# A ConvNeXt V2 block: one ring of four PSUM banks for the expansions, a new order inside the slot, and another pace of the recompute

## The chip, the cores and the metric

The kernel runs on one core of a Trainium2 chip. The core has five engines, each with its own instruction stream: TensorE (PE; its weight loads are a row of their own, PEld), VectorE (DVE), ScalarE (ACT), GpSimd (POOL) and SyncE (SP), which only issues transfers here. Matmuls write PSUM[...]; ACT and DVE read it. The engines wait for each other through semaphores. The metric is the time of one execution on the device in microseconds.

## The reference

The input is an image of 512 x 512 pixels with 96 channels in bf16.

```python
out = sum(xp[:, i:i+H, j:j+W, :] * dw[i, j] for i in range(3) for j in range(3))  # depthwise 3x3
h = layernorm(out)                          # over the 96 channels of each pixel
h = gelu(einsum('bhwc,ce->bhwe', h, w1))    # expansion to 384 channels
gx = sqrt((h * h).sum(axis=(1, 2)) + 1e-6)  # over ALL pixels, per channel
nx = gx / (gx.mean(axis=-1) + 1e-6)
h = grn_gamma * (h * nx) + grn_beta + h
return x + einsum('bhwe,ec->bhwc', h, w2)
```

The sum over all pixels in `gx` divides the work in two: no output can be made before every pixel has been expanded.

## The kernel before, in words

The image is cut into 128 blocks (`NBLK`) of four rows, 2048 pixels each. A block's pixels form four quarters of 512.

**Phase 1** walks through the blocks in slots (`for s in range(last_slot + 1)`, line 721). The convolution of block s runs in slot s; its normalisation follows some slots later, by way of statistics on PE, a Newton iteration on POOL and a trip through DRAM; and in most slots an earlier block is expanded (the "mlp" of that slot). There are 128 such expansions. The first few stand among slots that only convolve, then 114 in all have a convolution beside them, and the last 14 have none, because the convolutions have run out. Within a slot the order on each engine is the order in which the code calls the stages, since `InOrder` (line 22) keeps each engine's instructions in program order.

- The convolution of a block (`conv_taps`, line 408) is three bursts of 24 small matmuls into a tile Y of three banks. The first two bursts end in a `drain` of PE (line 441). `evac` copies Y to `y_bf` on ACT. In some early slots without expansion (`spare`) the result goes to two U tiles instead of Y.
- The expansion (`mlp_units`, line 611) makes twelve banks of 512 columns: `pair(j)` two quarters of 128 channels each, kept as `gsh`, for three groups of channels; `rest(n)` the remaining 3072 columns, kept as `gm`. A unit is some matmuls into a U tile followed by one GELU on ACT that empties it. `psU` has two buffers of two banks, so a unit's first matmul waits for the GELU of the unit before the last.
- Of the channel-major part (`gsh`, and the first 1536 columns of `gm` in two blocks of three), DVE takes the squares' sums with `bn_stats` (`squares`, `squares_rest`). The rest is pixel-major, and PE takes its squares as a Gram matrix (`gram_mms`, line 664): 12 matmuls in two blocks of three, 24 in the third, mostly one slot after the expansion.
- `stage_stats` makes the sums for the normalisation on PE; `stage_moments`, `stage_rstd`, `stage_newton` follow in later slots. Squares `ysq` and normalised `yn` are made on POOL.

Only the first quarter of `gsh` of a block is stored to DRAM (`g_dram`). The last two blocks stay resident.

**Phase 2** (from line 847) starts when the sums are complete and walks over the blocks again. Per block it adds the bias to x on POOL (`stage_xb`), recomputes the three quarters that weren't stored in three units (`recompute_units`: three matmuls into a tile U2, one GELU of 1536 columns), multiplies with the scaled w2 (`stage_mm2`, four sub-blocks of 12 matmuls each into O), adds on DVE and stores. The recompute of later blocks is mixed in between the sub-blocks by `pace` (line 330): it may run ahead by an allowance that starts at `LEAD` = 8 units and grows evenly, and at the end of each block it must at least have finished the next one. The six recompute units of the two resident blocks are made at the end of Phase 1, in `psU` (lines 843 to 845).

## Time and profile before

| | us |
|---|---|
| median of 11 runs | 1565.86 (one run of 7031.4, the others 1563.43 to 1570.16) |
| the profiled execution | 1567.04 |
| its span in the profile | 1565.3 |
| Phase 1 with convolution beside the expansion | about 114 to 945 |
| Phase 1 without convolution | about 945 to 1023 |
| Phase 2 | about 1032 to 1563 |

| engine | busy us | share of the span |
|---|---|---|
| PE | 1453.5 | 93% |
| ACT | 1446.9 | 92% |
| POOL | 1313.9 | 84% |
| DVE | 1129.8 | 72% |

The profile is of one execution. A busy PE is not PE at its peak, since matmuls overlap and their ends are modelled; the start of one to the start of the next says more. A group's row gives the busy time, the mean length of one instruction in nanoseconds, the idle time of its engine before it, and whose end finished most of that idle time. "PEclk" is the share of its full clock that TensorE was granted.

### The profile page before, as it was taken

What the parts mean: (1) busy time and instruction counts of PE and PEld (TensorE: products, weight loads), DVE (VectorE), ACT (ScalarE), POOL (GpSimd) and SP (SyncE); (2) the same over time, 40 slices, a digit from 0 to 9 for tenths busy, and PEclk for the clock granted to TensorE, in tenths of its full rate; (3) what the DMA queues carried; (4) which work ended last, traced back from release to release, by engine and by line L of the source; (5) the groups of instructions that cost most, each with busy time, mean ns of one, the idle gap of its engine ahead of it and who ended that gap; (6) DMA issues with size and microseconds to landing.
All of it is one profiled execution on the core that took longest, in us unless ns stands there. A gap on an engine that the chain in (4) does not pass through costs nothing. (4 is left out here: it accounts for less than half of the span.)

```text
span 1565.3 us, 55720 instructions
## 1 busy us (share of the span) xinstructions
PE 1453.5 (93%) x23749; PEld 844.7 (54%) x23749; DVE 1129.8 (72%) x2027; ACT 1446.9 (92%) x1306; POOL 1313.9 (84%) x933
## 2 busy tenths in 40 slices
PE   7889999999999999999999997789999999999997
PEld 3434444444444444444444444367777777777765
DVE  6738978889888888889888888855555555555544
ACT  3879999999999999999999999999999999999996
POOL 3558898988989898898889887559999999999994
PEclk8989999999999999999999999999999999999999
DMA  5668687787778778777778767779999999999993
GB/s 146 183 180 257 206 262 236 226 252 222 231 237 250 230 240 250 221 234 236 249 214 248 223 188 226 258 252 388 392 386 391 392 391 388 380 386 387 381 368 149
DMA packets 235470, 427.94 MB, mean 273 GB/s; under 512 B 34102, under 2 KB 148374, under 8 KB 235222
## 3 DMA queue, kind: packets, MB, share of 16 engines
q1 hardware_dynamic: 219972, 356.59, 70.2%
q0 software_dynamic: 13888, 67.64, 11.4%
q8 instruction: 186, 3.05, 0.8%
q14 instruction: 62, 0.51, 0.1%
q10 hardware_dynamic: 1362, 0.15, 0.1%
HBM read 272.78 MB, written 150.72 MB: 271 GB/s over the span
## 5 line engine op out<-in xcount | busy, mean ns | idle before, releaser
L32 PE MATMUL U<-ynT,w1p 128*128 128x512 bf16 x2166 | 602.1, 380 | 43.5 <-ACT gm L32 8.1
L32 DVE BATCH_NORM_STATS2 bst<-gsh 128x6 f32<-128x512 bf16 x756 | 468.8, 673 | 129.4 <-ACT gsh L32 128.8
L32 ACT ACTIVATE gr<-U 128x1536 bf16<-128x1536 f32 (+1 forms) x384 | 521.0, 1450 | 15.9 <-PE U L32 13.9
L32 POOL TENSOR_TENSOR yn<-y_bf,rbc 128x1536 bf16<-128x1536 bf16 x128 | 397.0, 3104 | 89.2 <-ACT rbc L32 30.4
L32 DVE TENSOR_TENSOR o_sb<-O,xb 128x384 bf16<-128x384 f32 x512 | 277.7, 557 | 252.0 <-PE O L32 180.1
L278 POOL TENSOR_TENSOR xb<-xr,B2c 128x1536 f32<-128x1536 bf16 x126 | 394.9, 3135 | 42.2 <-DVE B2c L32 34.0
L32 ACT ACTIVATE gsh<-U 128x1024 bf16<-128x1024 f32 x378 | 369.4, 1024 | 55.5 <-ACT gm L32 29.9
L32 ACT ACTIVATE gm<-U 128x1024 bf16<-128x1024 f32 x384 | 367.9, 1036 | 0.1
L32 PE MATMUL Y<-xT,Wq 64*32 64x511 bf16 (+1 forms) x8694 | 323.1, 391 | 9.3 <-DVE B2bc_f L32 3.7
L32 POOL TENSOR_TENSOR ysq<-y_bf 128x1536 bf16<-128x1536 bf16 x114 | 313.3, 2749 | 12.6 <-ACT y_bf L32 12.2
L32 PEld LDWEIGHTS <-w1p 128*128 128x128 bf16 x2166 | 169.1, 97 | 277.2 <-issue 173.1
L32 PEld LDWEIGHTS <-gr 128*128 128x128 bf16 x4584 | 228.6, 98 | 84.5 <-ACT gr L32 12.1
L32 PE MATMUL O<-W2s,gr 128*128 128x96 bf16 x4584 | 251.4, 206 | 12.1 <-ACT gr L32 9.4
L32 PEld LDWEIGHTS <-Wq 64*32 64x32 bf16 x9216 | 102.6, 91 | 189.6 <-issue 149.8
L32 PE MATMUL U<-w1p,ynT 128*128 128x384 bf16 (+2 forms) x1032 | 161.4, 272 | 34.1 <-ACT gm L32 31.0
L32 ACT ACTIVATE y_bf<-Y 128x1536 bf16<-128x1536 f32 x121 | 175.1, 1447 | 19.1 <-PE Y L32 18.9
L32 DVE STREAM_TRANSPOSE xT<-xin 128x576 f32<-128x576 f32 (+1 forms) x256 | 181.4, 748 | 5.9 <-PE Y L32 2.9
L32 DVE BATCH_NORM_STATS2 bst<-gm 128x6 f32<-128x512 bf16 x252 | 156.5, 677 | 0.9 <-ACT gm L32 0.9
L32 PEld LDWEIGHTS <-ynT 128*128 128x128 bf16 x1032 | 88.6, 96 | 91.4 <-issue 69.9
L32 PE MATMUL SG<-gm 128*128 128x128 bf16 x2064 | 136.3, 219 | 0.5 <-ACT gm L32 0.3
L32 PEld LDWEIGHTS <-gm 128*128 128x128 bf16 x2064 | 120.9, 98 | 11.5 <-issue 0.5
L250 POOL DMA_DIRECT2D xr<-in_x_dram x123 | 67.6, 549 | 27.6 <-POOL xb L278 27.6
(103 smaller groups left out, 702.7 us busy)
## 6 DMA issues: line engine op xcount, KB each, us to landing
ynT<-yn_dram SPq DMA_DIRECT2D x254, 384.0 KB
xin<-in_x_dram SPq DMA_DIRECT2D x126, 432.0 KB
yn_dram<-yn SPq DMA_DIRECT2D x512, 96.0 KB
xr<-in_x_dram POOLq DMA_DIRECT2D x128, 384.0 KB, 6.6
out_dram<-o_sb SPq DMA_DIRECT2D x127, 384.0 KB
g_dram<-gsh SPq DMA_DIRECT2D x126, 384.0 KB
gl<-g_dram SPq DMA_DIRECT2D x84, 384.0 KB
gl<-g_dram POOLq DMA_DIRECT2D x42, 384.0 KB, 6.6
```

The costliest lines, as they stand in the source:

```text
L32: r = f(*a, **k)
L250: pq.dma_start(out=xr[:], in_=x[0, r0:r0 + GR].rearrange("r w c -> (r w) c").rearrange("(p g) c -> p g c", g=PXP))
L278: pq.tensor_tensor(out=xb[:], in0=grp[q]["xr"][:], in1=bias[:, None, :].to_broadcast([128, PXP, C]), op=ALU.add)
```

## The change

There are four edits.

1. The two U buffers of two banks become one tile `ring` of four banks, allocated once. `banks(n)` returns the next n neighbouring banks of it, from the start again where they wouldn't fit. All users of `psU` take their banks from there: the expansions, the spare convolutions, `stage_spread`, the six resident recompute units.
2. `pair` and `rest` become `unit(bank, n)`, an expansion of one or two banks. The second pair and the last one are split into two single banks, so a slot with convolution has four units of two banks and four of one, with one GELU each.
3. The order inside a slot is another. With convolution: the Gram matmuls of the block before come in two halves between expansions; the evacuation of the convolution stands behind the fourth two-bank step, `unit(6, 2)`, where it stood behind `pair(2)`; the statistics come at the end; the drain after the second burst is gone. Without convolution: the Gram matmuls come after the second pair.
4. `pace` lets the allowance grow by `total` over the whole of Phase 2, not by `total + 2 - LEAD`.

```diff
-        psU = p1.enter_context(tc.tile_pool(name="psU", bufs=2, space=bass.MemoryType.PSUM))
+        psU = p1.enter_context(tc.tile_pool(name="psU", bufs=1, space=bass.MemoryType.PSUM))
+        NB = 4
+        ring = psU.tile([128, NB, W], f32, name="U")
+        next_bank = [0]
+
+        def banks(n):
+            k = next_bank[0] % NB
+            if k + n > NB:
+                k = 0
+            next_bank[0] = k + n
+            return ring[:, k:k + n, :]
...
-                    U = psU.tile([128, 2, QW], f32, name="U")
+                    U = banks(2)
...
-            even = LEAD + (n * NSUB + sub + 1) * (total + 2 - LEAD) / (NSUB * NBLK)
+            even = LEAD + (n * NSUB + sub + 1) * total / (NSUB * NBLK)
...
-                Ua = psU.tile([128, 2, W], f32, name="U")
-                Ub = psU.tile([128, 2, W], f32, name="U")
+                Ua, Ub = banks(2), banks(2)
...
-                if n < 2:
+                if n < 2 and fence:
                     pe.drain()
...
-            def pair(j):
-                U = psU.tile([128, 2, QW], f32, name="U")
-                for t in range(2):
-                    cm_mm(U[:, t, :], j, t)
-                act.activation(out=gsh[:, :, j, :], in_=U[:], func=ACTF.Gelu_apprx_tanh)
-
-            def rest(n):
-                U = psU.tile([128, 2, QW], f32, name="U")
...
+            def unit(bank, n):
+                U = banks(n)
+                if bank < 2 * NCH:
+                    j, t0 = divmod(bank, 2)
+                    for t in range(t0, t0 + n):
+                        cm_mm(U[:, t - t0, :], j, t)
+                    act.activation(out=gsh[:, t0:t0 + n, j, :], in_=U, func=ACTF.Gelu_apprx_tanh)
+                    return
...
-        def gram_mms(b):
-            for k in range((TAIL - px0(b)) // E):
+        def gram_mms(b, part=None):
+            n = (TAIL - px0(b)) // E
+            for k in range(n) if part is None else range(n // 2) if part == 0 else range(n // 2, n):
...
-                conv(0)
-                pair(0)
-                pair(1)
...
-                squares(0)
-                conv(1)
-                spread_out()
...
-                pair(2)
-                squares(1)
...
-                conv(2)
-                if evac:
+                if taps:
+                    conv(0)
+                    unit(0, 2)
+                    unit(2, 1)
+                    squares(0)
+                    conv(1, False)
+                    spread_out()
+                    if s + 2 < NBLK:
+                        turn_x(s + 2)
+                    unit(3, 1)
+                    unit(4, 2)
+                    squares(1)
+                    gram_of_last(0)
+                    unit(6, 2)
+                    squares(2)
+                    for k in get("turn"):
+                        stage_turn(k)
+                    conv(2)
                     evac()
-                rest(0)
-                squares(2)
...
-                rest(1)
...
-                rest(2)
-                squares_rest()
+                    gram_of_last(1)
+                    unit(8, 2)
+                    unit(10, 1)
+                    unit(11, 1)
+                    squares_rest()
+                    for b2 in get("stats"):
+                        stage_stats(b2)
+                else:
+                    unit(0, 2)
+                    unit(2, 2)
+                    spread_out()
+                    gram_of_last(0)
+                    gram_of_last(1)
+                    squares(0)
+                    unit(4, 2)
...
+                    unit(10, 2)
+                    squares_rest()
```

## The prediction

> **What bounds the kernel now.** I read the page's slices first: from about 110 us to 1023 us TensorE (PE) and ScalarE (ACT) are both nearly full, and after 1032 us too. A table of stretches then separates four stages (busy us of PE, PEld, DVE, ACT, POOL, each with its count; then clock, DMA share, GB/s):

> ```profile
> 114.00:945.00 831.00, 777.73 (x14078) 390.51 (x14075) 713.38 (x1210) 777.27 (x774) 736.74 (x558) 1.00 0.77 234
> 945.00:1023.00 78.00, 57.73 (x472) 33.26 (x470) 67.52 (x114) 74.52 (x81) 44.00 (x33) 1.00 0.80 259
> 1032.00:1466.00 434.00, 430.93 (x6094) 315.03 (x6094) 232.37 (x434) 430.25 (x318) 406.19 (x246) 1.00 1.02 381
> 1466.00:1563.00 97.00, 86.35 (x1183) 61.27 (x1179) 46.28 (x85) 84.12 (x61) 75.07 (x42) 1.00 0.79 289
> ```

> The first is Phase 1 with a convolution in every slot (PE 94%, ACT 94%); the second has no convolution left and is ACT's (96%); the third is Phase 2, PE and ACT at 99%; in the fourth ACT falls to 87%. The starts of the first GELU of each slot give the period: 7.45, 7.45, 7.64 us and again, mean 7.52, in Phase 1; 5.78 us on average in the 14 slots without convolution. The timeline of PE in one slot (start, duration, count; the bracket is idle time before it):

> ```profile
> 601.80 0.87 PE L32 MATMUL Y<-xT,Wq 64*32 64x512 bf16 x24
> 602.79 1.03 PE L32 MATMUL U<-ynT,w1p 128*128 128x512 bf16 x4
> 603.75 0.87 PE L32 MATMUL Y<-xT,Wq 64*32 64x512 bf16 x24
> 604.74 0.60 PE L32 MATMUL U<-ynT,w1p 128*128 128x512 bf16 x2
> 605.27 0.90 PE L32 MATMUL Y<-xT,Wq 64*32 64x512 bf16 x24
> 606.10 0.61 PE L32 MATMUL U<-w1p,ynT 128*128 128x384 bf16 x4
> ...
> 607.59 0.83 PE L32 MATMUL SG<-gm 128*128 128x128 bf16 x12
> 608.73 0.60 PE L32 MATMUL U<-w1p,ynT 128*128 128x256 bf16 x4 [0.31 <-ACT gm L32]
> ```

> PE stands back to back and waits for ACT once, 0.3 us. It can, because the two U buffers let it fill one while ACT empties the other.

> For the change the hand-over between them matters. It shows bare where ACT has nothing else, after the last slot: PE writes a pair, ACT empties it.

> ```profile
> 1018.86 0.59 PE L32 MATMUL U<-ynT,w1p 128*128 128x512 bf16 x2
> 1019.49 1.02 ACT L32 ACTIVATE resg<-U 128x1024 bf16<-128x1024 f32 x1 [0.62 <-PE U L32]
> 1020.57 0.60 PE L32 MATMUL U<-w1p,ynT 128*128 128x128 bf16 x4 [0.68 <-ACT resg L32]
> ```

> Start of a pair to start of its GELU: 0.63 us here, 0.69 at 602.79 with 603.48 on ACT; I take 0.66. The GELU takes 1.02, and PE starts 0.05 us after its end (1019.49+1.02=1020.51, 1020.57). So a pair handed over **in series** costs 0.66+1.02+0.05 = 1.73 us; a single bank, with one matmul of 0.215 us less and 512 columns of ACT, 0.45+0.59+0.05 = 1.09. The 0.59 is from:

> ```profile
> L32 ACT ACTIVATE y_bf<-Y 128x1536 bf16<-128x1536 f32 x121 | 175.1, 1447 | 19.1 <-PE Y L32 18.9 <-issue 0.2
> L32 ACT ACTIVATE y_bf<-U 128x512 bf16<-128x512 f32 x7 | 4.1, 591 | 0.0
> ```

> [...] its halved stretches are 6.83, 3.41 and 10.24 us long, whole windows. I measured each window's share of streaming from the matmul starts (512 columns each 0.215 us, eight convolution matmuls at once counted as one). All three windows that lost the clock streamed 0.30 or less; none at 0.38 or more did before the end. At half clock 0.69, 0.81 and 0.85 restored it, 0.65 and 0.68 did not. Two of these windows (clock is the third number from the end):

> ```profile
> 85.70:89.10 3.40, 1.77 (x48) 0.63 (x48) 0.00 (x0) 1.48 (x1) 2.78 (x1) 1.00 0.40 147
> 89.10:92.50 3.40, 3.28 (x79) 1.19 (x64) 1.75 (x5) 2.47 (x2) 1.54 (x5) 0.51 0.30 71
> ```

> **The change part by part.** (1) *The ring.* One tile U of four banks replaces two tiles of two banks. In the built program the first matmul of every unit waits for the ACTIVATE directly before it: u2 (bank 2) for u0's (banks 0 and 1), u3 (bank 3) for u2's, u4 for u3's, and so on; before, each waited for the last but one. Dependencies are kept for the tile, not for its banks. So PE and ACT take turns, and each slot becomes one chain. With t=0 at u0's first matmul:

> - u0 0, evacuated by 1.68, u2 1.73; evacuated 2.77.
> - The second burst runs 0.31 after u2's start (as 604.96 to 605.27) for 0.83: u3 at 2.87, evacuated 3.91; u4 3.96, evacuated 5.64; u6 5.69, evacuated 7.37.
> - The third burst fits behind u6; y_bf starts on ACT at 7.3 and holds it 1.35 (next start at 606.32 to 607.66): ACT is free at 8.65. Second Gram half and u8's matmuls are done by then, so u8's GELU runs 8.65 to 9.67.
> - u10 9.72, evacuated 10.76; u11 10.81.
> - Behind u11's matmuls stand the statistics (0.60, from 606.55 to 607.15) and the first burst of the next slot with its drain (0.99): 10.81+0.22+0.60+0.99 = 12.6.

> **12.6 us against 7.52, at full clock.** The slots without convolution are six pairs in series, 6 x 1.73 = 10.4 plus 0.1 for long Gram blocks, against 5.78.

> (2) *Clock.* In this chain PE streams little. From u8 to the end of u11's matmuls (7.5 to 11.1) it streams 0.43+0.21+0.21 us, 0.13 to 0.28 of any window lying there: below every window that lost the clock before. At half clock I work the chain out again with a pair's second matmul at 0.43 and a matmul's length of 0.61 (pair 1.13 to ACT, single 0.70), bursts of 1.39 and 1.54 (90.54 to 95.15 is three): 17.3 us. There the stretch from u4 to u8 streams over 0.69 of a window, so the clock comes back once a slot, to be lost again near u11 or, where a block has 24 Gram matmuls, later. Following the window's edges through a few slots gives 15 to 16.7; I take **15.4** as mean. Without convolution no cold window reaches 0.69: six pairs at 2.20 and Gram of double length make 13.7.

> (3) *Splits of two pairs into singles*: two more ACTIVATEs a slot, price inside the chain. (4) *Evacuation behind the fourth expansion*: y_bf comes one unit later; it hides u8's matmuls. POOL's square of it and the norm come slots later, DVE and POOL have over 5 us more per slot, so nothing waits there. (5) *Gram halves*: 0.35 or 0.70 us each, nothing, because ACT's 1.02 us on u4 and the burst behind u6 cover them; without that cover 0.7 or 1.4. (6) *Statistics at the end*: on the chain, 0.60, counted; the moments on DVE come after them in the next slot as before. (7) *Second drain gone*: bursts with it take 0.98, without 0.83 (605.27 to 606.10): saves 0.15, of which the chain feels at most 0.1. DMA queues are not reordered within a slot.

> (8) *Pace of Phase 2.* The allowance grows by 384/512 instead of 378/512 a sub-block, so the lead no longer runs out. Before, lead minus need is 4.95 - 0.047n units and is gone at block 105. The last output addition of each block shows that: mostly 4.0 to 4.2 us apart until 1470 us, then 4.46, 4.64 and 5.53. PE there waits for a GELU inside the block. Twenty blocks from 1469.9 to 1562.1 took 92.2; at 4.10 they take 82, and I count **11 us** gained with the tail, between 5 and 18: POOL needs 3.13 (xb) + 0.55 (xr's issue) + gaps, 4.0 a block, and sets the floor.

> Sum on the profiled execution (span 1565.3, 1567.0 around it; the median of runs, 1565.86, is a microsecond less):

> - 114 slots with convolution x (15.4-7.52) = +898
> - 14 slots without x (13.7-5.78) = +111
> - six resident recompute pairs in series +8, first stages (spare convolutions, spreads through one ring) +5
> - Phase 2 -11

> 1567+1011 = 2578; I say **2580**.

> **The rivals.** *B: serial at full clock.* If ping-pong at this rate counts as busy, 114 x 5.08 = 579, 14 x 4.7 = 66, +6 +5 -11: **2212**. For it: pairs every 0.92 us at 1024 us kept the clock at 0.44 to 0.47 streaming. Against: the new chain has windows at half of that. *C: cold almost throughout*: 114 x 9.8 + 111 + 2: **2795**; against it the dense stretch u4 to u8. *D, the other side: PE is let in as soon as its own banks are free.* Then the ring works as a finer double buffer. Place: the first matmul of each unit; price: a slot is PE's own work, 7.45-0.44-0.15 = 6.86, or 7.49 with 24 Gram matmuls, mean 7.07, so 114 x -0.45 - 11 gives **1505**. It decides from the point where a unit waits for the ACTIVATE before last; the built program waits for the last, which is why I give it little.

> **How the numbers follow.** A 0.65, B 0.22, C 0.10, D 0.03. A spreads from 14 to 16.7 us a slot, 2400 to 2740. The range takes in B's lower side and A's upper: 2205 to 2760. Differences within 0.2% (3 us) can't be told from none by these runs: faster 0.03 from D, same 0.01, slower 0.96.

> **What would show it.** U matmuls waiting for ACT and ACT for U about seven times a slot, over 3 us a slot each; slots of 12.6 (B) or 15 to 16.7 (A); a mean clock near 0.7 from 100 us on (A), 0.99 (B); DVE and POOL near half busy; Phase 2 of about 519 us with no block above 4.7. Slots near 7 us, or U's matmuls starting while the previous unit's ACTIVATE runs, would make all of it wrong; a clock that follows another measure than streaming moves me between B and C.

## The result and the profile after

The changed kernel takes **2500.87 us** (median of 8 runs, 2494.42 to 2502.09) against 1566.0: 1.596 times as long, interval 1.594 to 1.598. The forecast was 2580, range 2205 to 2760. The profiled execution has a span of 2499.1 us and a mean granted clock of 0.779.

The table of stretches of the changed kernel (busy us of PE, PEld, DVE, ACT, POOL, each with its count; then clock, DMA share, GB/s) has Phase 1 with convolution, Phase 1 without, and Phase 2:

```profile
150.00:1765.00 1615.00, 1125.08 (x13996) 481.11 (x13993) 741.52 (x1195) 847.97 (x981) 732.00 (x544) 0.73 0.38 119
1765.00:1950.00 185.00, 105.48 (x553) 56.59 (x551) 76.76 (x120) 89.67 (x89) 44.89 (x33) 0.57 0.36 115
1967.00:2496.00 529.00, 514.79 (x7272) 374.38 (x7271) 278.09 (x516) 511.78 (x377) 482.94 (x287) 1.00 1.00 365
```

ACT was at 94% in the first stretch and is at 53% now, PE fell from 94% to 70%, and the clock is at 0.73. Phase 2 is as long as before. The table of waits says what stands in between (total us, times, longest):

```profile
ACT gsh L32 <- PE U L32: 589.1, 490, 3.3
PE U L32 <- ACT gm L32: 291.2, 271, 1.7
PE U L32 <- ACT gsh L32: 285.1, 330, 1.4
ACT gm L32 <- PE U L32: 270.7, 384, 1.4
```

In the kernel before the same waits were these; the fourth, of `gm` for PE, is not in the list, and all idle time in front of these GELUs was 0.1 us:

```profile
PE U L32 <- ACT gm L32: 39.7, 112, 1.3
ACT gsh L32 <- PE U L32: 23.8, 46, 0.6
PE U L32 <- ACT gsh L32: 5.2, 11, 0.7
```

Now PE waits for ACT 576 us and ACT for PE 860 us: they take turns. The starts of the matmuls say the same without a wait being put down to anyone. In the 110 slots with convolution that the table below counts, the changed kernel's trace has 1832 matmuls into U, and not one starts while ACT reads U. Before, 1153 of 1829 do.

The timeline of PE in a slot that ran at full clock up to its last unit:

```profile
1624.71 0.60 PE L32 MATMUL U<-ynT,w1p 128*128 128x512 bf16 x2
1626.48 0.38 PE L32 MATMUL U<-ynT,w1p 128*128 128x512 bf16 x1 [1.16 <-ACT gsh L32]
1626.79 0.88 PE L32 MATMUL Y<-xT,Wq 64*32 64x512 bf16 x24
1627.60 0.39 PE L32 MATMUL U<-ynT,w1p 128*128 128x512 bf16 x1
1628.67 0.59 PE L32 MATMUL U<-ynT,w1p 128*128 128x512 bf16 x2 [0.69 <-ACT gsh L32]
...
1630.38 0.59 PE L32 MATMUL U<-ynT,w1p 128*128 128x512 bf16 x2 [0.78 <-ACT gsh L32]
...
1634.39 0.38 PE L32 MATMUL U<-w1p,ynT 128*128 128x256 bf16 x2 [1.66 <-ACT gm L32]
1635.45 0.58 PE L32 MATMUL U<-w1p,ynT 128*128 128x128 bf16 x2 [0.69 <-ACT gm L32]
...
1636.59 1.48 PE L32 MATMUL Y<-xT,Wq 64*32 64x512 bf16 x24
```

From the first line on, the units start at 1.77, 2.89, 3.96, 5.67, 9.68 and 10.74 us; the forecast's chain had 1.73, 2.87, 3.96, 5.69, 9.72 and 10.81. The last line is the first burst of the next slot at half clock: 1.48 us where it took 0.87.

```profile
1604.40:1607.80 3.40, 1.38 (x19) 1.00 0.84 262
1607.80:1611.20 3.40, 3.01 (x48) 0.51 0.03 10
...
1614.60:1618.00 3.40, 2.71 (x17) 0.50 0.00 0
1618.00:1621.50 3.50, 2.35 (x41) 0.99 0.93 294
```

PE's busy time is more than what it streams, which is counted here as in the prediction. The first holds units 10 and 11 with their waits and streams less than 0.3 of the window; the third holds units 4 and 6 and half of a long Gram block at half clock, and streams 0.82.

| stage | before, us | after, us | change | forecast |
|---|---|---|---|---|
| start to the first steady slot (first GELU of `gm`) | 114.4 | 143.8 | +29 | +36 |
| 110 slots with convolution | 829.9 | 1633.2 | +803 | +867 |
| 14 slots without, resident recompute, sums | 89.4 | 191.2 | +102 | +119 |
| Phase 2, first to last addition | 528.5 | 526.8 | -2 | -11 |

(Starts in the trace; of the forecast, four of the 114 slots and the 5 us of the first stages are put to the first row.) The mean slot with convolution is 14.85 us where 15.4 was forecast, the one without 12.9 where it was 13.7.

### The profile page after: what moved, and what is told of

Its sections match the earlier page's. It is cut to its first block, busy times and chain, and to the rows that moved or that the text cites. A ratio compares the mean times of both kernels' runs of the same rounds, so it can differ in the third digit from the quotient of the medians.

```text
span 2499.1 us, 55852 instructions
## 1 busy us (share of the span) xinstructions
PE 1865.4 (75%) x23749; PEld 961.8 (38%) x23749; DVE 1172.0 (47%) x2027; ACT 1538.5 (62%) x1534; POOL 1318.0 (53%) x933
## 4 chain that ended last, share of the span: by engine, by line
PE 57%; ACT 28%; POOL 7%; issue 4%; DMA 2%; DVE 1%; SPq 1%; ACTq 0%; POOLq 0%
PE U L32 30%; PE Y L32 13%; ACT gsh L32 12%; ACT gm L32 10%; PE O L32 7%; PE SG L32 6%; ACT y_bf L32 6%; POOL xb L289 6%; DMA yn_dram<-yn 2%; SPq L32 1%; POOL gl L256 1%; DVE o_sb L32 1%; POOL xr L261 0%; DMA xin<-in_x_dram 0%; ACT gr L32 0%
## 5 line engine op out<-in xcount | busy, mean ns | idle before, releaser
L32 PE MATMUL U<-ynT,w1p 128*128 128x512 bf16 x2166 | 779.0, 449 | 308.2 <-ACT gsh L32 260.3
L32 DVE BATCH_NORM_STATS2 bst<-gsh 128x6 f32<-128x512 bf16 x756 | 489.0, 680 | 779.0 <-ACT gsh L32 774.3
L32 POOL TENSOR_TENSOR ysq<-y_bf 128x1536 bf16<-128x1536 bf16 x114 | 313.0, 2746 | 870.9 <-ACT y_bf L32 846.5
L32 ACT ACTIVATE gsh<-U 128x1024 bf16<-128x1024 f32 x492 | 406.5, 826 | 591.1 <-PE U L32 589.1
L32 ACT ACTIVATE gm<-U 128x1024 bf16<-128x1024 f32 x498 | 412.6, 829 | 271.3 <-PE U L32 270.7
L32 ACT ACTIVATE gr<-U 128x1536 bf16<-128x1536 f32 (+1 forms) x384 | 520.1, 1455 | 19.3 <-PE U L32 18.5
L32 PE MATMUL Y<-xT,Wq 64*32 64x511 bf16 (+1 forms) x8694 | 437.1, 512 | 8.2 <-DVE B2bc_f L32 3.7
L32 POOL TENSOR_TENSOR yn<-y_bf,rbc 128x1536 bf16<-128x1536 bf16 x128 | 395.6, 3093 | 75.8 <-ACT rbc L32 30.9
L32 PE MATMUL U<-w1p,ynT 128*128 128x384 bf16 (+2 forms) x1032 | 214.6, 315 | 293.6 <-ACT gm L32 266.5
L32 DVE TENSOR_TENSOR o_sb<-O,xb 128x384 bf16<-128x384 f32 x512 | 277.5, 556 | 250.5 <-PE O L32 148.1
L32 PEld LDWEIGHTS <-w1p 128*128 128x128 bf16 x2166 | 188.8, 105 | 483.0 <-issue 422.2
L32 PEld LDWEIGHTS <-gr 128*128 128x128 bf16 x4584 | 236.2, 98 | 107.9 <-issue 22.7
L32 PE MATMUL O<-W2s,gr 128*128 128x96 bf16 x4584 | 256.6, 206 | 12.9 <-DVE o_sb L32 12.4
L32 PEld LDWEIGHTS <-Wq 64*32 64x32 bf16 x9216 | 112.5, 102 | 396.0 <-issue 372.4
L32 PEld LDWEIGHTS <-ynT 128*128 128x128 bf16 x1032 | 108.4, 110 | 392.5 <-issue 369.5
L32 DVE BATCH_NORM_STATS2 bst<-gm 128x6 f32<-128x512 bf16 x252 | 166.4, 688 | 147.1 <-ACT gm L32 147.1
L32 PEld LDWEIGHTS <-gm 128*128 128x128 bf16 x2064 | 183.5, 126 | 124.7 <-issue 117.5
L32 PE MATMUL SG<-gm 128*128 128x128 bf16 x2064 | 219.6, 272 | 0.0
L32 ACT ACTIVATE y_bf<-Y 128x1536 bf16<-128x1536 f32 x121 | 175.2, 1448 | 38.0 <-PE Y L32 37.3
L32 DVE STREAM_TRANSPOSE xT<-xin 128x576 f32<-128x576 f32 (+1 forms) x256 | 181.2, 747 | 9.0 <-PE Y L32 6.5
```

Source lines behind the costliest of these rows:

```text
L32: r = f(*a, **k)
```

## The experiments

**The ring alone.** The kernel before, with its own order and units, gets its U banks from the ring:

```diff
...
-                U = psU.tile([128, 2, QW], f32, name="U")
+                U = banks(2)
...
```

> Only the ring in the kernel before: its old order, its pairs and rests of two banks, its pace. Serial hand-over theory: each unit waits for the ACTIVATE right before it, the slot is a chain of six pairs with the evacuation between: p0 0, p1 1.73, p2 3.46, y_bf on ACT 5.05 to 6.4, rest 0 emptied by 7.42, rest 1 7.47, rest 2 9.20, next p0 10.93 us. 114 x (10.93-7.52) + 14 x 4.7 + 11 = about +466, so 2030 us. PE streams over 0.40 of every window in that chain, so the clock should stay near full. Rival, that the new order and the splits cost the time and the ring does not: about 1566.

Measured: 2113.26 us, 1.350 times before (1.346 to 1.354). The ring by itself costs 547 us, and again none of 1832 matmuls into U starts while ACT reads U. Its undisturbed slots take 10.83 to 10.91 us, worked out 10.93. What was missed is the clock: it was lost in the slots without convolution, which take 12.97 us and not 10.4, and in some others (11.7 to 12.5 us); 338 us ran at half clock from the first steady slot on, mean 0.91. The rival that the ring costs nothing falls. The changed kernel's slots at full clock are 1.7 us longer than these: in series, the splits and the new order cost too.

**The ring alone taken back.** The changed kernel, with two tiles of two banks in turn:

```diff
-        psU = p1.enter_context(tc.tile_pool(name="psU", bufs=1, space=bass.MemoryType.PSUM))
-        NB = 4
-        ring = psU.tile([128, NB, W], f32, name="U")
-        next_bank = [0]
+        psU = p1.enter_context(tc.tile_pool(name="psU", bufs=2, space=bass.MemoryType.PSUM))
...
-            return ring[:, k:k + n, :]
+            return psU.tile([128, 2, W], f32, name="U")[:, :n, :]
```

> The changed kernel with the ring alone taken back: each unit takes one of two tiles of two banks in turn; order, splits, Gram halves and pace as changed. Serial hand-over theory: the loss is gone, PE's own work (6.9 to 7.5 us a slot) or ACT's (6.9) sets the slot, 1510 to 1555 us, clock 0.99. Rival, that the order costs: well above 1600.

Measured: 1768.58 us, 1.131 times before (1.128 to 1.134), clock 0.977. So 732 of the 935 us are gone, but not all: most slots take 9.01 to 9.26 us. A single bank now occupies a whole tile, so unit 11 has to wait for unit 8's GELU. First ACT, then PE in one slot:

```profile
622.16 2.11 ACT L32 ACTIVATE gm<-U 128x1024 bf16<-128x1024 f32 x3
625.85 3.22 ACT L32 ACTIVATE gsh<-U 128x1024 bf16<-128x1024 f32 x4 [1.58 <-PE U L32]
```

```profile
623.25 0.38 PE L32 MATMUL U<-w1p,ynT 128*128 128x128 bf16 x2 [1.61 <-ACT gm L32]
623.47 0.44 PE L32 MATMUL SG<-rowsel,y_bf 128*128 128x4 bf16 x12
...
625.16 0.82 PE L32 MATMUL U<-ynT,w1p 128*128 128x512 bf16 x3
```

Behind unit 11 PE has the statistics and a burst to do, 1.9 us until unit 0, and ACT has only one GELU of 0.6 us left to live on; it idles 1.6 us in each slot. That loss belongs to the splits in this form, as the next two runs show, which leave them out (and have the second drain back, 0.15 us of PE's time by the lines of the prediction); in the changed kernel itself the chain is another, and it can't be taken as a share of its 935 us.

**Pairs instead of splits**, in two tiles and the changed order, with both drains; and the same with all loads of `gl` on SP's queue:

```diff
-                    unit(2, 1)
+                    unit(2, 2)
...
-                    conv(1, False)
+                    conv(1)
...
-                    unit(3, 1)
...
-                    unit(10, 1)
-                    unit(11, 1)
+                    unit(10, 2)
```

> Two tiles of two banks, the new order, all units of two banks, both drains, the new pace, loads of gl as before. Against the same with the loads on SP: 8 to 12 us more if POOL sets Phase 2. If the new order lets PE run through, 1510 to 1535; if not, 1563 to 1567.

> Two tiles of two banks, the new order of the slot, all units of two banks (no splits), both drains, the new pace, and the loads of gl all on SP's queue. If the new order lets PE run without waiting for ACT: slots of 7.0 to 7.2 us for 7.52, 36 to 55 us less; if POOL sets the floor of Phase 2, another 8 to 12 less: 1500 to 1525. If the old order was as good: 1550 to 1566.

Measured: 1578.83 us (ratio 1.008, 1.006 to 1.010) and 1561.68 us (0.997, 0.996 to 0.998). The first is above both of its ranges, the second lies in the one for an order no better than the old. Between them are 17 us, where 8 to 12 were expected for the loads. Most slots take 7.38, 7.32 and 7.55 us, a little under the 7.45, 7.46, 7.64 of before and not the 7.0 to 7.2 expected. And each twelfth takes about 9.5, the one after it about 8.4. The trace of the second kernel shows why, on PE and on DVE:

```profile
632.87 0.60 PE L32 MATMUL U<-ynT,w1p 128*128 128x512 bf16 x2
635.25 0.49 PE L32 MATMUL SG<-gm 128*128 128x128 bf16 x6 [1.77 <-DVE SG L32]
...
636.45 1.48 PE L32 MATMUL Y<-xT,Wq 64*32 64x512 bf16 x24
```

```profile
632.02 2.76 DVE L32 BATCH_NORM_AGGREGATE mv<-bst 128x2 f32<-128x192 f32 x3
634.70 0.23 DVE L32 TENSOR_SCALAR mom<-SG 128x128 f32<-128x128 f32 x1
635.03 0.17 DVE L32 MEMSET SG<- 128x128 f32 x1
```

The Gram sums and the statistics are different columns of one tile, SG. In the changed order the first Gram half comes early in a slot; in one slot of twelve the memset of the statistics stands on DVE behind three aggregations, and PE waits 1.8 us for it. The clock is lost there too: the burst after the pause takes 1.48 us, as at half clock, where the one before it took 0.88, and the mean clock is 0.985, against 0.994 in the next run, without the wait.

**The aggregations behind the moments**, in the second of these kernels:

```diff
             for k in get("moments"):
                 stage_moments(k)
+            for b in owed:
+                combine(b)
+            owed = []
...
-            for b in get("combine"):
-                combine(b)
+            owed = get("combine")
...
```

> As the kernel with two tiles, pairs, the new order and gl on SP, but the three aggregations of each 12th slot come after the moments of the next slot on DVE, so that the memset of the sums' bank does not wait for them and the Gram matmuls not for the memset. If that wait is what made pairs of slots of 9.5 and 8.4 us every 12 slots: they fall to 7.3 to 7.6, 10 times 3 us less than 1562, so about 1532. If not, 1562.

Measured: 1535.26 us, 0.981 of before (0.978 to 0.983) and 26 us less than with the wait; steady slots of 7.31 to 7.58 us. The wait was the cause.

**Zeros in the gaps.** The changed kernel with matmuls of zeros added to the Gram sums, in two doses; adding zeros leaves the sums as they are. This is the small dose.

```diff
                     unit(8, 2)
+                    fill(22)
                     unit(10, 1)
+                    fill(11)
                     unit(11, 1)
```

> The changed kernel, with 22 matmuls of zeros into the Gram sums behind the matmuls of unit 8 and 11 behind those of unit 10, where PE waits for ACT (they add nothing, and fit in the gaps of 1.7 and 0.7 us). Clock theory: the low window is gone, slots with convolution fall from 14.87 to 12.6 us, slots without stay at 12.9; 2501 - 114 x 2.27 = 2240 us, and the clock rises from 0.78 to over 0.9. Rival, that the lost clock is only a companion of the waits: 2500 or more, with the extra matmuls on top.

> The changed kernel with matmuls of zeros into the Gram sums in every gap in which PE waits for ACT: 18 behind unit 0, 12 behind unit 3, 22 behind unit 8, 11 behind unit 10, and 18 behind each unit of the slots without convolution. Clock theory: the clock stays at 0.97 or more, slots with convolution are 12.6 to 12.9 us and those without 10.4 to 10.7; the whole takes what the prediction worked out for a serial chain at full clock, without its gain in Phase 2, and 0 to 30 us for the zeros: 2225 to 2255. If slots of 15.8 us stay, the clock is not what lengthens them.

Measured: 2340.75 us with the small dose, clock 0.894, and about 470 instead of about 1060 us at half clock in Phase 1: the direction was right, but other windows still lose it, and slots of 12.85 and 14.47 us alternate. With the large dose 2225.94 us and clock 0.995:

```profile
145.00:1500.00 1355.00, 1205.23 (x20493) 787.86 (x20493) 723.07 (x1177) 828.45 (x966) 720.12 (x540) 1.00 0.45 140
```

Slots with convolution are 12.60 to 12.74 us, those without 11.06. More work made the kernel 275 us faster. So the loss divides: **about 275 us for the clock that the waits cost, and about 660 us that stay at full clock**, for the hand-over in series with the splits and the order that it makes dear. What the zeros cost by themselves is in the 660: slots without convolution take 11.06 us, where six pairs in series were put at 10.4 to 10.5.

**A tile for each bank.** Four tiles of one bank replace the ring, every unit of two banks becomes two of one:

```diff
-        ring = psU.tile([128, NB, W], f32, name="U")
...
+        psU = p1.enter_context(tc.tile_pool(name="psU", bufs=4, space=bass.MemoryType.PSUM))
+
+        def bank():
+            return psU.tile([128, W], f32, name="U")[:]
...
-                    conv(1, False)
+                    conv(1)
...
```

> Four tiles of one bank in place of the ring, so that each bank has its own waits; every unit of two banks becomes two of one, with two GELUs; the changed order, both drains, the changed pace. Serial theory: with waits for each bank the hand-over overlaps again; ACT needs 12 x 0.48 + 1.35 = 7.1 us a slot, or more where a wait shows, so slots of 7.3 to 7.8 and 1550 to 1610 us. If the new order itself costs time as with two tiles and splits (9.0 us a slot), 1740 or more.

Measured: 1558.25 us, 0.995 of before (0.993 to 0.997); slots of 7.67, 7.17 and 7.22 us, with the pair of 8.1 and 7.4 in each twelfth. With the same four banks, in the same order but for the second drain, which is back, and with twelve GELUs a slot instead of eight, the 935 us are gone and 8 are gained. PE and ACT overlap again: 1110 of 1834 matmuls into U start while ACT reads U. What matters is which waits each bank has.

**The pace alone, `gl` on SP alone, and both**, on the kernel before:

```diff
-            even = LEAD + (n * NSUB + sub + 1) * (total + 2 - LEAD) / (NSUB * NBLK)
+            even = LEAD + (n * NSUB + sub + 1) * total / (NSUB * NBLK)
...
-                (pq if q % 3 == 0 else sq).dma_start(
+                sq.dma_start(
```

> The kernel before with the new pace alone. The step of the prediction: 11 us less (5 to 18), 1555. Rival, read from the changed kernel's profile: POOL's queue sets the length of Phase 2 (blocks of 4.01, 4.03 and 4.50 us, the long one with a load of gl on POOL), so the stall at the end only moves: 1563 to 1567.

> All loads of gl on SP's queue, with the old pace. POOL theory: the end still collapses when the lead is gone, because there PE and ACT wait for each other and not for POOL; 0 to 4 us less, 1562 to 1566. If POOL alone were the bound: as much less as with the new pace, 1552 to 1556.

> The new pace and all loads of gl on SP's queue. POOL theory: POOL saves 0.55 us in each third block, blocks fall to about 4.03 us, 126 x 0.16 = 20 us at most, 10 to 14 expected since the first third of Phase 2 was not POOL's: 1552 to 1556. Rival, that PE and ACT or the transfers set the length: 1563 or more.

Measured: 1566.17 (0.9996, 0.9985 to 1.0007), 1562.16 (0.997, 0.996 to 0.998) and 1549.23 us (0.988, 0.986 to 0.990). With the pace alone the blocks of 4.6 to 5.5 us at the end are gone, and blocks of 4.02, 4.03 and 4.50 us stand in their place from the second third of Phase 2 on (one takes 7.03). POOL's timeline there:

```profile
1403.42 3.13 POOL L278 TENSOR_TENSOR xb<-xr,B2c 128x1536 f32<-128x1536 bf16 x1
1406.84 0.56 POOL L250 DMA_DIRECT2D xr<-in_x_dram  x1 [0.30 <-POOL xb L278]
1407.40 0.54 POOL L245 DMA_DIRECT2D gl<-g_dram  x1
1407.95 3.13 POOL L278 TENSOR_TENSOR xb<-xr,B2c 128x1536 f32<-128x1536 bf16 x1
```

POOL has no gap in these lines but the 0.30 us in front of xr's issue: 3.13+0.30+0.56 is 4.0 us a block, 4.5 with a load of gl, 4.18 on average. PE and ACT need 4.03, as the kernel with both edits shows, whose blocks are that long but for the last three. First the stretch with the pace alone, then with both (busy us of PE, PEld, DVE, ACT, POOL):

```profile
1240.00:1500.00 260.00, 249.60 (x3504) 179.79 (x3502) 131.43 (x246) 252.43 (x186) 237.61 (x146) 1.00 1.02 373
```

```profile
1240.00:1500.00 260.00, 260.00 (x3680) 191.38 (x3678) 143.87 (x258) 260.00 (x195) 235.25 (x129) 1.00 1.04 392
```

Before, POOL fell behind too: `xb` was ready 4 us ahead of its addition in the first blocks and just in time from block 52 on. The stall at the end gave it time to catch up, to 6 us ahead. Each cure alone leaves the other bound (with the loads on SP alone the blocks at the end still take 4.5 to 5.5 us), and the two together bring 17 us where they bring 0 and 4 apart.

**All together**, with the four tiles:

> Four tiles of one bank, the changed order and pace, with the loads of gl on SP's queue and the aggregations behind the moments. If the three gains add: slots of 7.2 to 7.7 us without the one of 8.1 in each twelfth (12 us less than with four tiles alone) and blocks of 4.03 us in Phase 2 (15 less): 1530 us, a few under the 1535 of the two tiles. If the finer hand-over brings nothing beyond two tiles: 1535 or more.

Measured: 1532.78 us, 0.980 of before (0.978 to 0.981). Slots are 7.66, 7.17 and 7.23 us without the long ones, blocks 4.03. The gains add, within 2 us. Against the two tiles (1535.26) it is 2.5 us less, which these runs can't tell from none.

## Why the prediction was right, and where it wasn't

- **The ring is serial: right, and shown.** The ring alone costs 547 us with everything else as before; a tile for each bank takes the whole loss away with the changed order (the second drain apart, and each unit in single banks). The sign that was to make it wrong, a matmul into U while ACT reads U, does not occur once with the ring; with the four tiles it does in 1110 of 1834, so it is the one tile that makes the hand-over serial, not the four banks. The price of a hand-over (1.73 and 1.09 us) gave 12.6 us a slot at full clock, and 12.60 to 12.74 were measured once the clock was held.
- **The clock is lost: right.** With zeros in the gaps the time falls by 275 us. Rival B's 2212 is what the kernel takes without the loss, 2226; it failed because the clock was not kept at this rate of hand-overs, 0.73 in the first stretch. Rival C's clock was too low, since the stretch from unit 4 to unit 8 does bring it back: in the windows above it streams 0.82, and the clock goes from 0.50 to 0.99.
- **How much of a slot is cold: mis-sized.** Following the window's edges by hand gave 15.4 us as the mean; it was 14.85. I took each slot to lose the clock once. In the locked pattern one slot of three does not: the one with 24 Gram matmuls wins the clock back at its unit 6 (1618.1 us) and keeps it until unit 10 of the next slot (1635.1 us), 17.07 us. The 12.63 us between these two slots' first GELUs of `gm` lie in that stretch and are as long as a slot at full clock. Units 10 and 11 of the slot that keeps the clock fall into a window that holds no Gram matmul and streams 0.38 (1621.5 to 1624.9), because it also takes in the next slot's first burst; in the slot after, unit 10 stands at the end of a window that streams less than 0.3. By this count it is where the windows' edges fall that decides in these two slots; what the long Gram block does to the pattern was not tested apart. The 110 slots account for 64 of the 77 us by which the sum was too long (867 against 803). The first slots and those without convolution were too long as well, and the 9 us that Phase 2 did not gain hid a part of it, which is luck.
- **Slots without convolution: mis-sized.** 13.7 was for half clock throughout; they took 12.9, at a mean clock of 0.57: some 11 us.
- **The pace: the step that failed.** "POOL needs 3.13 (xb) + 0.55 (xr's issue) + gaps, 4.0 a block, and sets the floor": this left out the load of gl which POOL issues in each third block. The floor was 4.18, above PE's and ACT's 4.03, so the 11 us became 2 in the changed kernel's profile and none in the comparison of the pace alone. The stall at the end was real, but it was not what set the length of Phase 2 by itself.
- **Edits costed at nothing: right at this chain, not in general.** Gram halves and the later evacuation lie behind ACT's time in the changed kernel. Where the hand-over overlaps, the early Gram half meets DVE's memset: a wait of 1.8 us in each twelfth slot, which with the clock that it costs makes that slot and the next about 3 us longer together, 26 us in all. I had looked at DVE and said that the moments come as before; what comes earlier is the reader of the memset.
- **Rival D's mechanism** exists once each bank is a tile, but the price was 7.35 us a slot (the last kernel), not 7.07. D counted PE's own work alone; in that kernel it is ACT, with a GELU for each bank, that has no time left: from 300 to 800 us it is busy 496 us, PE 476. What D would cost with the eight GELUs of the changed kernel, no run shows. (The sum for rival C comes to 2797 with the 1567 that the others start from, not 2795.)

The pieces of the forecast make +1011 us, the trace has +934.

## What to carry to other kernels

A ring inside one tile has one set of waits: each writer waits for the last reader of any part of it, and a double buffer turns into turn-taking. Give each part that is to be reused by itself a tile of its own, and read the waits of the built program before believing in an overlap. Where a stall vanishes and the time does not, look for an engine that had used the stall to catch up, and count all it issues, transfers too.

## What the runs showed of the hardware that I had not expected

- PE lost its clock though it was never idle for long: in the steady slots of the changed kernel its longest idle time was 1.7 us. Counting streaming from the matmul starts, all 100 windows of 3.413 us that lost the clock streamed less than 0.4, and the 306 that kept it about 0.35 or more. At half clock the 99 that won it back had about 0.65 or more, the 225 that didn't about 0.8 or less. In between the windows of each pair overlap, and a few hundredths depend on how the shortest matmuls are counted; but the two levels lie apart, and the clock of this run changed 199 times.
- The swing locks: six slots in 26 windows for some 20 slots, then three slots in 13 windows for some 60, with one break.
- 63 matmuls of zeros a slot (90 where there is no convolution) held the clock at 0.995, where it was 0.779, and took 11% off the time.
